# Gathering a chunk's small matmuls: one run of all scores and one of all outputs per chunk, in place of a run per unit

## The chip, the cores and the metric

The kernel runs on one core of one Trainium2 chip. The time is microseconds (us) of device time of one execution. A measurement is the median of several runs.

## The reference

A decayed linear attention, block by block with a carried state, feeds a two-layer network with a softplus between the layers. With B, H, S, D = 4, 8, 768, 64 and blocks of 64 rows:

```python
for b in range(nb):
    intra = np.einsum('bhic,bhjc->bhij', qb, kb) * Dmask[None]
    intra = np.einsum('bhij,bhjd->bhid', intra, vb)
    inter = np.einsum('bhid,bhde->bhie', qb * lam_pow[None], kv_state)
    out[:, :, sl] = intra + inter
    kb_dec = kb * rev_pow[None]
    kv_state = lam_block[None, :, None, None] * kv_state + np.einsum('bhsd,bhse->bhde', kb_dec, vb)
...
h = x @ w_in                                   # (3072, 512) @ (512, 2048)
g = np.maximum(h, 0.0) + np.log1p(np.exp(-np.abs(h)))
return (g @ w_out).astype(np.float32)          # (2048, 512)
```

## The kernel before

The sequence is cut into 6 chunks of 128 rows (`NCH`), each of two blocks of 64 rows. A chunk's attention is cut into 4 units (`NP`), each with two heads for all four batches; unit `g` belongs to chunk `g // 4`. A unit's q, k, k transposed and v come in one SBUF tile `att` of 1 MB in all, which the SyncE queue (SP) loads in two halves of 512 KB (`load_upto`, L86 to L89).

**Attention of a unit.** Chunk 0 has code of its own. For the later chunks, TensorE does 64x64 matmuls in fp32. `mm_scores` (L269 to L280) writes the scores into bank `x` (L276) and the state sums into bank `y` (L278). VectorE masks the scores (L297, into the tile of k) and updates the state with four `scalar_tensor_tensor` (L302). ScalarE first scales the transposed k (`k_decay`, L262), VectorE scales q (`q_decay`, L267). `mm_out` (L282 to L293) writes the unit's output `z` into the two banks of the `work` tile: L289 adds the part from the state, L293 the part from the masked scores. ScalarE copies `z` to the high half of x (`x_high`, L318), VectorE subtracts for the low half (`x_low`, L325). Every fp32 number is split into a high and a low fp32r half, so that each product of the network takes three matmuls.

**The network.** Per chunk there are 16 steps (`NF`), one per 128 columns of `w_in`. Step `s` does `mlp1(s)` (L353, 12 matmuls of 128x128 by 128x512 into a bank `h`), then softplus (ScalarE, L334), the high half (ScalarE, L338) and the low half (VectorE, L342), and 4 steps later (`LAG`) `mlp2` (L370, 12 matmuls) adds into the four `o` banks of the chunk. After a chunk's last `mlp2` the four banks are copied (ScalarE and VectorE, L376) and stored by SP (L378).

**The order** is written by hand: every engine executes its instructions as the code issues them. Up to step 16 a list of words sets it (the string before the loop), which also converts the weights. From step 17 a loop does it: at every fourth step an "event" `g` does the outputs of unit `g - 1` and at once the scores of unit `g` (`out1`, `sc1`), and then `mask`, `update_states`, `q_decay`, one extra `mlp2`, and asks for unit `g + 1`. So TensorE changes from large to small matmuls and back at each event: four times in the list for units 4 to 8, the last of them for units 7 and 8, and 16 times in the loop.

**PSUM** has 8 banks: four `o`, two `h`, two in `work`. SBUF tiles of 8 KB a partition (`b8`) number 22, of which 16 hold the weights.

Of the kernel before, what the change touches and what calls it, by code (L numbers as in the profile page):

```python
# [31 lines left out]
def decay_attention_softplus_ffn(  # L32
# [47 lines left out]
    def load_half(g, major):  # L80
        nc.sync.dma_start(out=unit(g)[:, major], in_=att[g // NP, g % NP, :, major])
# [4 lines left out]
    def load_upto(n):  # L86
        for g in range(len(units), min(n, NG)):
            for major in range(2):
                load_half(g, major)  # L89

# [56 lines left out]

    keep_warm(13)

# [131 lines left out]

    def mm_out(g, w):  # L282
        a, qd, v, st = k_of(g), q_of(g), vt_of(g), states[g]
        for b in range(B):
            cols = slice(b * 64, b * 64 + 64)
            for s in range(2):
                r = half(s)
                for t in range(2):
                    nc.tensor.matmul(w[half(t), s, cols], lhsT=st[r, b, t], rhs=qd[r, b, t], start=True, stop=False)  # L289
            for s in range(2):  # L290
                r = half(s)
                for t in range(2):
                    nc.tensor.matmul(w[half(t), s, cols], lhsT=v[r, b, t], rhs=a[r, b, t], start=False, stop=True)  # L293

# [13 lines left out]
    def update_states(g, y):  # L308
        u = y.rearrange("q (b t e) -> q b t e", b=B, t=2)
        st = states[g]  # L310
        decayed(g, st[hi], st[lo], lo, u[hi])
        if not last_chunk(g):
            states[g + NP] = th([128, B, 2, D], F32, f"st_{g + NP}")
            decayed(g, states[g + NP][lo], st[hi], hi, u[lo])

    def x_high(g, w):
# [41 lines left out]
    def mlp2(ss):  # L358
        c = ss[0] // NF
        ends = ss[-1] % NF == NF - 1  # L360
        if ss[0] % NF == 0:
            o_tiles[c] = [obank(f"o{c}_{b}") for b in range(B)]
        if ends:
            ob = t8([128, B, 512], F32, f"ob{c}")
        for b in range(B):
            for s in ss:
                f = s % NF
                g, w = g_tiles[s], w_of(f, 1)
                for n, (i, j) in enumerate(((0, 0), (0, 1), (1, 0))):
                    nc.tensor.matmul(  # L370
                        o_tiles[c][b], lhsT=g[:, i, b * 128 : (b + 1) * 128], rhs=w[:, j],
                        start=f == 0 and n == 0, stop=f == NF - 1 and n == 2,
                    )
            if ends:
                copy = nc.vector.tensor_copy if b % 2 else nc.scalar.copy
                copy(out=ob[:, b], in_=o_tiles[c][b])  # L376
                queue = nc.scalar if c == NCH - 1 and b % 2 == 0 else nc.sync
                queue.dma_start(out=out[b * S + c * C : b * S + (c + 1) * C, :], in_=ob[:, b])  # L378

# [82 lines left out]
    def out1(g):  # L462
        z[g] = work(f"z{g}")
        mm_out(g, z[g])

# [10 lines left out]
    for line in """  # L476
# [23 lines left out]
        glo 11, mlp 12, lo 22 23, sign 24 25, add 24 25, act 12, out1 6, sc1 7, m1 7, scale 26 27, shift 26  # L500
        27, ghi 12, round 28 29, hi 24 25, glo 12, kd1 8, sign 26 27, lo 24 25, mlp2 9, xh1 6, shift 28 29,
        mlp 13, load 32, round 26 27, act 13, add 26 27, scale 30 31, sign 28 29, hi 26 27, add 28 29, lo 26
        27, xl1 6, mlp2 10, mlp 14, hi 28 29, ghi 13, glo 13, round 30 31, mlp2 11, shift 30 31, act 14, qd
        7, ghi 14, glo 14, up 7, mlp 15, lo 28 29, act 15, sign 30 31, out1 7, ghi 15, sc1 8, up 8, add 30
        31, mlp2 12, mlp2 13, m1 8, xh1 7, unit 10, xl1 7, hi 30 31, mlp 16, lo 30 31, qd 8, glo 15
    """.replace("\n", " ").split(","):
# [8 lines left out]
    last = NCH * NF  # L515
    events = {s: 2 * NP + (s - NF) // 4 for s in range(NF, last - NF + 1, 4)}
    ahead = 17 - LAG
    for s in range(17, last + LAG):
        if events.get(s + 1, NG) < NG:
            run("kd1", events[s + 1])  # L520
        if s - 1 < last:
            chain_act(s - 1)
            chain_hi(s - 1)
            chain_lo(s - 1)
        if s == last + LAG - 2:
            mlp2([s - LAG, s - LAG + 1])
        elif s - LAG < last - 1 and ahead != s - LAG:
            mlp2([s - LAG])
        if s in events:
            g = events[s]  # L530
            run("out1", g - 1)
            if g < NG:
                run("sc1", g)
            run("xh1", g - 1)
            if g < NG:
                run("m1", g)
            if s % NF == 0:
                run("xl1", g - 1)
            if g < NG:
                run("up", g)  # L540
            if s % NF:
                run("xl1", g - 1)
            if g < NG:
                run("qd", g)
            ahead = s - LAG + 1
            mlp2([ahead])
            load_upto(g + 2)
        if s < last:
            mlp1(s)
# [37 lines left out]
```

## Time and profile before

| what | value |
|---|---|
| median of three runs | 595.82 us (595.77 to 595.89) |
| the profiled execution | 595.62 us; its span, first to last instruction, 593.8 us |
| TensorE matmuls, busy | 586.9 us, 99% of the span, 5009 records |
| TensorE weight loads, busy | 484.3 us, 82% |
| VectorE, ScalarE, busy | 224.3 us (38%), 210.0 us (35%) |
| granted TensorE clock | 1.000 over the span |
| DMA | 48.95 MB, mean 82 GB/s |

PE stands for TensorE's matmuls, PEld for its weight loads, DVE for VectorE, ACT for ScalarE. A written matmul of fp32 operands appears as two records of a matmul and two of a weight load (L276 has 640 matmul records for 20 units of 16 written ones); one of fp32r operands appears as one of each. The windows view gives, for a stretch of time, the busy time and the number of instructions (also those that only reach into it) of each engine, the granted clock, the mean busy share of the 16 DMA engines and the GB/s moved.

### The profile page before, as it was taken

What the parts mean: (1) busy time and instruction counts of PE and PEld (TensorE: products, weight loads), DVE (VectorE), ACT (ScalarE), POOL (GpSimd) and SP (SyncE); (2) the same over time, 40 slices, a digit from 0 to 9 for tenths busy, and PEclk for the clock granted to TensorE, in tenths of its full rate; (3) what the DMA queues carried; (4) which work ended last, traced back from release to release, by engine and by line L of the source; (5) the groups of instructions that cost most, each with busy time, mean ns of one, the idle gap of its engine ahead of it and who ended that gap; (6) DMA issues with size and microseconds to landing.
All of it is one profiled execution on the core that took longest, in us unless ns stands there. A gap on an engine that the chain in (4) does not pass through costs nothing.

```text
span 593.8 us, 11190 instructions
## 1 busy us (share of the span) xinstructions
PE 586.9 (99%) x5009; PEld 484.3 (82%) x5009; DVE 224.3 (38%) x338; ACT 210.0 (35%) x341; POOL 1.5 (0%) x9
## 2 busy tenths in 40 slices
PE   8999999999999999999999999999999999999997
PEld 6778888888888888888888888888888888888885
DVE  8999999623313134132232331312312211211011
ACT  5899867232233232322323213323232222222211
POOL 1000000000000000000000000000000000000000
PEclk9999999999999999999999999999999999999999
DMA  8999230214002106001022300220500000100001
GB/s 288 416 416 418 106 131 2 72 73 142 3 0 72 73 0 214 0 2 52 21 72 90 124 3 0 73 72 0 214 0 2 1 0 1 72 0 2 0 1 71
DMA packets 15759, 48.95 MB, mean 82 GB/s; under 512 B 1888, under 2 KB 1888, under 8 KB 15712
## 3 DMA queue, kind: packets, MB, share of 16 engines
q1 hardware_dynamic: 15344, 47.46, 21.4%
q10 hardware_dynamic: 368, 0.79, 0.4%
q8 instruction: 39, 0.64, 0.4%
q14 instruction: 8, 0.07, 0.0%
HBM read 41.95 MB, written 6.29 MB: 81 GB/s over the span
## 4 chain that ended last, share of the span: by engine, by line
PE 94%; DMA 3%; DVE 1%; SPq 1%; issue 0%; ACT 0%
PE o L370 45%; PE h L353 42%; PE x L276 2%; PE z L289 2%; PE z L293 2%; DMA att<-in_att 1%; DMA raw<-in_wts 1%; PE y L278 1%; DVE c L219 1%; DVE w L232 0%; DVE c L215 0%; DVE c L225 0%; PE y L440 0%; SPq L122 0%; PE w L276 0%
## 5 line engine op out<-in xcount | busy, mean ns | idle before, releaser
L370 PE MATMUL o<-w,g 128*128 128x512 f32 x1152 | 278.6, 392 | 0.0
L353 PE MATMUL h<-x,w 128*128 128x512 f32 x1152 | 274.5, 390 | 0.3 <-ACT x L417 0.3
L353 PEld LDWEIGHTS h<-x,w 128*128 128x128 f32 x1152 | 215.8, 188 | 46.4 <-DVE w L232 0.7
L370 PEld LDWEIGHTS o<-w,g 128*128 128x128 f32 x1152 | 214.8, 188 | 45.3
L342 DVE TENSOR_TENSOR g<-l,g 128x512 fp32r<-128x512 f32 x96 | 66.4, 692 | 305.3 <-ACT g L338 305.3
L334 ACT ACTIVATE l<-h 128x512 f32<-128x512 f32 x96 | 57.5, 598 | 310.9 <-PE h L353 308.6
L338 ACT CAST g<-l 128x512 fp32r<-128x512 f32 x96 | 59.6, 621 | 2.8
L302 DVE SCALAR_TENSOR_TENSOR st<-st,lam_c,y 64x256 f32<-64x256 f32 x68 | 29.9, 480 | 2.4 <-PE y L278 1.3
L297 DVE TENSOR_TENSOR att<-x,mask 128x512 f32<-128x512 f32 x19 | 13.1, 692 | 43.4 <-PE y L278 23.8
L318 ACT CAST x<-z 128x512 fp32r<-128x512 f32 x20 | 11.7, 585 | 41.4 <-PE z L293 41.4
L289 PEld LDWEIGHTS z<-att,st 64*64 64x64 f32 x640 | 17.0, 134 | 7.0 <-issue 6.3
L276 PE MATMUL x<-att 64*64 64x64 f32 x608 | 21.7, 219 | 0.0
L278 PE MATMUL y<-att 64*64 64x64 f32 x544 | 21.3, 219 | 0.0
L289 PE MATMUL z<-att,st 64*64 64x64 f32 x640 | 20.9, 224 | 0.0
L225 DVE CUSTOM_DVE_ANT_0 c<-raw,c 128x2048 uint16<-128x2048 uint16 (+1 forms) x19 | 20.0, 1054 | 0.3
L276 PEld LDWEIGHTS x<-att 64*64 64x64 f32 x608 | 20.1, 135 | 0.0
L232 DVE TENSOR_TENSOR w<-c,w 128x1024 fp32r<-128x1024 f32 (+1 forms) x19 | 20.0, 1055 | 0.1
L219 DVE SCALAR_TENSOR_TENSOR c<-raw,c 128x1024 uint32<-128x1024 uint32 (+1 forms) x19 | 20.0, 1053 | 0.0
L207 ACT ACTIVATE c<-raw 128x1024 f32<-128x1024 f32 (+1 forms) x19 | 18.9, 1006 | 3.1 <-DMA raw<-in_wts 3.1
L293 PE MATMUL z<-att 64*64 64x64 f32 x640 | 19.9, 218 | 0.0
L278 PEld LDWEIGHTS y<-att 64*64 64x64 f32 x544 | 19.6, 135 | 0.0
L211 ACT ACTIVATE raw<-raw 128x1024 uint32<-128x1024 uint32 (+1 forms) x19 | 19.1, 1013 | 1.2 <-DMA raw<-in_wts 1.2
(48 smaller groups left out, 172.6 us busy)
## 6 DMA issues: line engine op xcount, KB each, us to landing
att<-in_att SPq DMA_DIRECT2D x43, 512.0 KB, 4.9
raw<-in_wts SPq DMA_DIRECT2D x32, 512.0 KB, 9.2
out_dram<-ob SPq DMA_DIRECT2D x22, 256.0 KB, 2.3
att<-in_att SPq DMA_DIRECT2D x9, 256.0 KB, 7.5
out_dram<-ob ACTq DMA_DIRECT2D x2, 256.0 KB, 2.0
att<-in_att ACTq DMA_DIRECT2D x1, 256.0 KB, 4.7
lam_b<-in_lam SPq DMA_DIRECT2D x1, 4.0 KB, 2.8
```

Source lines behind the costliest of these rows:

```text
L219: nc.vector.scalar_tensor_tensor(out=c, in0=raw_at(ks, 1), scalar=0x80000000, in1=c, op0=ALU.bitwise_and, op1=ALU.bitwise_or)
L225: nc.vector.tensor_add(out=c, in0=c, in1=raw_at(ks, 0))
L276: nc.tensor.matmul(x[r, cols], lhsT=k[r, b, t], rhs=q[r, b, t], start=True, stop=True)
L278: nc.tensor.matmul(y[half(1 - s), cols], lhsT=kd[r, b, t], rhs=v[r, b, t], start=True, stop=True)
L289: nc.tensor.matmul(w[half(t), s, cols], lhsT=st[r, b, t], rhs=qd[r, b, t], start=True, stop=False)
L293: nc.tensor.matmul(w[half(t), s, cols], lhsT=v[r, b, t], rhs=a[r, b, t], start=False, stop=True)
L302: nc.vector.scalar_tensor_tensor(out=to[:, :, t], in0=of[:, :, t], scalar=lam_c[r, h : h + 1], in1=u[:, :, t], op0=ALU.mult, op1=ALU.add,)
L334: nc.scalar.activation(l_tiles[s], h_tiles.pop(s), AF.Softplus)
L338: nc.scalar.copy(out=g_tiles[s][:, 0, :], in_=l_tiles[s])
L342: nc.vector.tensor_sub(out=g[:, 1, :], in0=l_tiles.pop(s), in1=g[:, 0, :])
L353: nc.tensor.matmul(h_tiles[s], lhsT=w[:, i, cs], rhs=x[:, j, :], start=p == 0 and n == 0, stop=p == NP - 1 and n == 2,)
L370: nc.tensor.matmul(o_tiles[c][b], lhsT=g[:, i, b * 128 : (b + 1) * 128], rhs=w[:, j], start=f == 0 and n == 0, stop=f == NF - 1 and n == 2,)
```

## The change

Nothing of the arithmetic of chunks 1 to 5 changes. What changes is where the small matmuls of chunks 2 to 5 stand, and into which banks they write.

- **One run of scores per chunk.** At the fourth step of a chunk (`f == LAG - 1`), right behind the last `mlp2` of the chunk before, `chunk_scores` does the scores and state sums of all four units of the next chunk: into the two `h` banks, the four `o` banks (two units) and `work`. Behind it VectorE masks and updates for four units on end. The state of the chunk is kept in the unit's own tile, in the place of the transposed k (`update_kept`), for which ScalarE copies half of the old state.
- **One run of outputs per chunk.** At step 8 of a chunk (step 11 of the last but one) `chunk_outs` does the outputs of all four units of the next chunk: units 0 and 1 into the two `h` banks, units 2 and 3 into `work`. Four casts and four subtractions of 512 columns follow.
- **Loads.** From unit 8 on a unit is one transfer of 1 MB. Two units are asked for at a chunk's step 1 and two behind `chunk_outs`.
- **Stores.** The tile for a chunk's results is split in two of the `b4` tiles.
- **The `mlp2` order** follows `mlp2_upto`: none at step 4 of a chunk, two at step 5, one extra ahead of `chunk_outs`.
- **The start.** 13 large warm-up matmuls become 9 large and 34 small ones of 64x64 on zeros.
- **The list** loses `kd1 8`, `sc1 8`, `up 8`, `m1 8`, `qd 8`.

TensorE, in the middle of chunk 1, before: `z10` is the output of unit 10, `x11` and `y11` the scores and sums of unit 11, `o1_` the banks of `mlp2`, `h` those of `mlp1`.

```order
L370 MATMUL o1_3_1435<-w10_948,g24_1756 128x512 x3
L289 MATMUL z10_1851<-att10_1537,st_10_944 64x64 x4
L293 MATMUL z10_1851<-att10_1537 64x64 x4
...
L276 MATMUL x11_1884<-att11_1738 64x64
L278 MATMUL y11_1885<-att11_1738 64x64
...
L370 MATMUL o1_0_1432<-w11_997,g25_1774 128x512 x3
L370 MATMUL o1_1_1433<-w11_997,g25_1774 128x512 x3
L370 MATMUL o1_2_1434<-w11_997,g25_1774 128x512 x3
L370 MATMUL o1_3_1435<-w11_997,g25_1774 128x512 x3
L353 MATMUL h28_1943<-x_1_0_711,w10_948 128x512 x6
```

Now, the run of scores at chunk 2's step 3 (`x12` to `y15` are units of chunk 3, unit 15 in the `work` tile `w15`), and the run of outputs at its step 8 (`z3_0`, `z3_1` in the `h` banks, `z3_2568` in `work`):

```order
L422 MATMUL o1_3_1616<-w15_1307,g31_2104 128x512 x3
L290 MATMUL x12_2233<-att12_1887 64x64
L292 MATMUL y12_2234<-att12_1887 64x64
...
L290 MATMUL w15_2335<-att15_2134 64x64
L292 MATMUL w15_2335<-att15_2134 64x64
L405 MATMUL h35_2396<-x_2_0_1877,w1_295 128x512 x6
...
L422 MATMUL o2_3_2436<-w7_753,g37_2477 128x512 x3
L303 MATMUL z3_0_2566<-att12_1887 64x64 x2
L303 MATMUL z3_1_2567<-att12_1887 64x64 x2
...
L307 MATMUL z3_2568<-att15_2134 64x64 x4
L405 MATMUL h40_2711<-x_2_0_1877,w6_604 128x512 x6
```

A run of 128 pairs of a weight load and a matmul, of two units, has become two runs of 256 pairs, of four units each (192 in the scores of the last chunk), and of four places in a chunk at which TensorE changes to small matmuls two are left.

VectorE at the same place, before, at one event (`att13` masked, two states updated, `x_3_0` the low half, `att13` the scaled q):

```order
L342 TENSOR_TENSOR g35_2248<-l35_2246,g35_2248 128x512
L297 TENSOR_TENSOR att13_2141<-x13_2300,mask_104 128x512
L302 SCALAR_TENSOR_TENSOR st_13_1520<-st_13_1520,lam_c_108,y13_2301 64x4x64 x2
L302 SCALAR_TENSOR_TENSOR st_17_2339<-st_13_1520,lam_c_108,y13_2301 64x4x64 x2
L325 TENSOR_TENSOR x_3_0_2334<-z12_2267,x_3_0_2334 128x2x4x64
L267 TENSOR_TENSOR att13_2141<-att13_2141,lp_105 128x512
L342 TENSOR_TENSOR g36_2374<-l36_2372,g36_2374 128x512
```

and now, behind the run of scores:

```order
L428 COPY ob1_1_2212<-o1_3_1616 128x512
L311 TENSOR_TENSOR att12_1887<-x12_2233,mask_135 128x512
L316 SCALAR_TENSOR_TENSOR att12_1887<-st_12_1552,lam_c_139,y12_2234 64x4x64 x2
L316 SCALAR_TENSOR_TENSOR st_16_2372<-att12_1887,lam_c_139,y12_2234 64x4x64 x2
L311 TENSOR_TENSOR att13_1889<-x13_2267,mask_135 128x512
...
L311 TENSOR_TENSOR att15_2134<-w15_2335,mask_135 128x512
L316 SCALAR_TENSOR_TENSOR att15_2134<-st_15_1573,lam_c_139,w15_2335 64x4x64 x2
L316 SCALAR_TENSOR_TENSOR st_19_2393<-att15_2134,lam_c_139,w15_2335 64x4x64 x2
L394 TENSOR_TENSOR g35_2411<-l35_2409,g35_2411 128x512
L281 TENSOR_TENSOR att12_1887<-att12_1887,lp_136 128x512
```

Five instructions that stood apart for each unit now stand on end for four units, ahead of the low half `g35`.

The diff, cut to its core:

```diff
     def load_upto(n):
         for g in range(len(units), min(n, NG)):
-            for major in range(2):
-                load_half(g, major)
+            if g < 2 * NP:
+                for major in range(2):
+                    load_half(g, major)
+            else:
+                nc.sync.dma_start(out=unit(g), in_=att[g // NP, g % NP])
...
-    keep_warm(13)
+    warm_h = bank("warm_h")
+
+    def keep_warm_small(n):
+        zero = warm.bitcast(F32)
+        for k in range(n):
+            r, other = half(k % 2), k // 2 % 2
+            c = half((k + other) % 2)
+            nc.tensor.matmul((warm_ps, warm_h)[other][c, :64], lhsT=zero[r, :64], rhs=zero[r, :64], start=True, stop=True)
+
+    keep_warm(9)
+    keep_warm_small(34)
...
+    def update_kept(g, y):
+        u = y.rearrange("q (b t e) -> q b t e", b=B, t=2)
+        old, st = states[g], kt_of(g)
+        states[g] = st
+        nc.scalar.copy(out=st[lo], in_=old[lo])
+        decayed(g, st[hi], old[lo], lo, u[hi])
+        if not last_chunk(g):
+            states[g + NP] = th([128, B, 2, D], F32, f"st_{g + NP}")
+            decayed(g, states[g + NP][lo], st[hi], hi, u[lo])
+
+    def chunk_scores(c):
+        homes = [(bank, bank), (obank, obank), (obank, obank), None]
+        for g, home in zip(range(c * NP, c * NP + NP), homes):
+            if home:
+                xy[g] = [new(f"{name}{g}") for new, name in zip(home, "xy")]
+            else:
+                w = work(f"w{g}")
+                xy[g] = w[:, 0], w[:, 1]
+            mm_scores(g, *xy[g])
+
+    def chunk_outs(c):
+        homes = {0: [bank(f"z{c}_{s}") for s in range(2)]}
+        w = work(f"z{c}")
+        homes[1] = [w[:, s] for s in range(2)]
+        for p in range(NP):
+            mm_out(c * NP + p, homes[p // 2], p % 2 * 256)
+        for i in range(2):
+            x_of(c, 2 * i)
+            x = x_tiles[c, i].rearrange("q n p (b s i) -> q n s p b i", b=B, s=2)
+            of = [home.rearrange("q (p b i) -> q p b i", p=2, b=B) for home in homes[i]]
+            for s in range(2):
+                nc.scalar.copy(out=x[:, 0, s], in_=of[s])
+            for s in range(2):
+                nc.vector.tensor_sub(out=x[:, 1, s], in0=of[s], in1=x[:, 0, s])
...
-            ob = t8([128, B, 512], F32, f"ob{c}")
+            ob = [t4([128, 2, 512], F32, f"ob{c}_{i}")[:, j] for i in range(2) for j in range(2)]
...
     for s in range(17, last + LAG):
-        if events.get(s + 1, NG) < NG:
-            run("kd1", events[s + 1])
+        c, f = divmod(s, NF)
+        first = (c + 1) * NP
+        if f == 1 and c < NCH - 1:
+            load_upto(first + NP)
+        if 1 <= f <= 3 and c < NCH - 1:
+            for g in ((first,), (first + 1,), (first + 2, first + 3))[f - 1]:
+                run("kd1", g)
...
+        if f != LAG or c == NCH:
+            mlp2_upto(s - LAG)
+        if f == LAG - 1 and c < NCH - 1:
+            chunk_scores(c + 1)
+            for g in range(first, first + NP):
+                mask_scores(g, xy[g][0])
+                update_kept(g, xy[g][1])
+        if f in range(LAG, 2 * LAG) and c < NCH - 1:
+            run("qd", first + f - LAG)
+        if f == (11 if c == NCH - 2 else 8) and c < NCH - 1:
+            if c < NCH - 2:
+                mlp2_upto(s - LAG + 1)
+            chunk_outs(c + 1)
+            mlp2_upto(s - LAG + 1)
+            load_upto(first + NP + 2)
         if s < last:
             mlp1(s)
```

More of the change, by code (lines that the diff above doesn't have):

```diff
@@ L280, in mm_scores, with mm_out @@
                         )
-    def mm_out(g, w):
+    def mm_out(g, w, first=0):
         a, qd, v, st = k_of(g), q_of(g), vt_of(g), states[g]
         for b in range(B):
-            cols = slice(b * 64, b * 64 + 64)
+            cols = slice(first + b * 64, first + b * 64 + 64)
             for s in range(2):
@@ L288, in mm_out @@
                 for t in range(2):
-                    nc.tensor.matmul(w[half(t), s, cols], lhsT=st[r, b, t], rhs=qd[r, b, t], start=True, stop=False)
+                    nc.tensor.matmul(w[s][half(t), cols], lhsT=st[r, b, t], rhs=qd[r, b, t], start=True, stop=False)
             for s in range(2):
@@ L292, in mm_out @@
                 for t in range(2):
-                    nc.tensor.matmul(w[half(t), s, cols], lhsT=v[r, b, t], rhs=a[r, b, t], start=False, stop=True)
+                    nc.tensor.matmul(w[s][half(t), cols], lhsT=v[r, b, t], rhs=a[r, b, t], start=False, stop=True)
     def mask_scores(g, x):
@@ L375, in mlp2 @@
                 copy = nc.vector.tensor_copy if b % 2 else nc.scalar.copy
-                copy(out=ob[:, b], in_=o_tiles[c][b])
+                copy(out=ob[b], in_=o_tiles[c][b])
                 queue = nc.scalar if c == NCH - 1 and b % 2 == 0 else nc.sync
-                queue.dma_start(out=out[b * S + c * C : b * S + (c + 1) * C, :], in_=ob[:, b])
+                queue.dma_start(out=out[b * S + c * C : b * S + (c + 1) * C, :], in_=ob[b])
     def w_group(j):
@@ L463, in out1 @@
         z[g] = work(f"z{g}")
-        mm_out(g, z[g])
+        mm_out(g, [z[g][:, s] for s in range(2)])
     step = {
@@ L500, in decay_attention_softplus_ffn @@
         glo 11, mlp 12, lo 22 23, sign 24 25, add 24 25, act 12, out1 6, sc1 7, m1 7, scale 26 27, shift 26
[L501 to L505, printed above, removed]
+        27, ghi 12, round 28 29, hi 24 25, glo 12, sign 26 27, lo 24 25, mlp2 9, xh1 6, shift 28 29, mlp 13,
+        load 32, round 26 27, act 13, add 26 27, scale 30 31, sign 28 29, hi 26 27, add 28 29, lo 26 27, xl1
+        6, mlp2 10, mlp 14, hi 28 29, ghi 13, glo 13, round 30 31, mlp2 11, shift 30 31, act 14, qd 7, ghi
+        14, glo 14, up 7, mlp 15, lo 28 29, act 15, sign 30 31, out1 7, ghi 15, add 30 31, mlp2 12, mlp2 13,
+        xh1 7, unit 10, xl1 7, hi 30 31, mlp 16, lo 30 31, glo 15
     """.replace("\n", " ").split(","):
@@ L515, in decay_attention_softplus_ffn, with mlp2_upto @@
     last = NCH * NF
-    events = {s: 2 * NP + (s - NF) // 4 for s in range(NF, last - NF + 1, 4)}
-    ahead = 17 - LAG
-    for s in range(17, last + LAG):
-        if events.get(s + 1, NG) < NG:
-            run("kd1", events[s + 1])
+    done = 17 - LAG
+    def mlp2_upto(n):
+        nonlocal done
+        while done < n:
+            ss = [done + 1] if done + 1 < last - 2 else [done + 1, done + 2]
+            if ss[-1] > n:
+                break
+            mlp2(ss)
+            done = ss[-1]
+    for s in range(17, last + LAG):
+        c, f = divmod(s, NF)
[5 more added lines that the diff above has]
+                run("kd1", g)
         if s - 1 < last:
@@ L524, in decay_attention_softplus_ffn @@
             chain_lo(s - 1)
[L525 to L547, printed above, removed]
+        if f != LAG or c == NCH:
[13 more added lines that the diff above has]
+            load_upto(first + NP + 2)
         if s < last:
```

## The prediction

> **What bounds the kernel now.** I read the page first: busy shares, then the chain that ended last.
>
> ```profile
> PE 586.9 (99%) x5009; PEld 484.3 (82%) x5009; DVE 224.3 (38%) x338; ACT 210.0 (35%) x341; POOL 1.5 (0%) x9
> PE 94%; DMA 3%; DVE 1%; SPq 1%; issue 0%; ACT 0%
> L370 PE MATMUL o<-w,g 128*128 128x512 f32 x1152 | 278.6, 392 | 0.0
> L353 PE MATMUL h<-x,w 128*128 128x512 f32 x1152 | 274.5, 390 | 0.3 <-ACT x L417 0.3
> ```
>
> TensorE is the bound: it is in 94% of the chain, and its groups have next to no idle time ahead of them. So a change pays only if TensorE has less to do or passes from one thing to the next faster. A busy time of 392 ns overlaps its neighbours, so I take cadences from the timeline of PE, in one stretch of the loop:
>
> ```profile
> 194.00 2.88 PE L353 MATMUL h<-x,w 128*128 128x512 f32 x12
> 196.72 2.88 PE L370 MATMUL o<-w,g 128*128 128x512 f32 x12
> ...
> 205.25 0.30 PE L289 MATMUL z<-att,st 64*64 64x64 f32 x8
> 205.37 0.30 PE L293 MATMUL z<-att 64*64 64x64 f32 x8
> 205.48 0.30 PE L289 MATMUL z<-att,st 64*64 64x64 f32 x8
> 205.60 0.30 PE L293 MATMUL z<-att 64*64 64x64 f32 x8
> ```
>
> Twelve large matmuls start 2.72 us before the next twelve: 226.7 ns each. Eight small ones take 0.117 us (0.35 us over three rows): 14.6 ns each. The windows view, cut at one stretch of large matmuls and the run of small ones behind it, and the timeline at the last run, which has outputs alone:
>
> ```profile
> 182.99:204.97 21.98, 21.98 (x102) 17.94 (x97) 6.51 (x11) 5.69 (x10) 0.00 (x0) 1.00 0.28 96
> 204.97:207.02 2.05, 2.05 (x130) 1.98 (x129) 0.00 (x0) 0.58 (x1) 0.00 (x0) 1.00 0.02 6
> ...
> 493.52 0.34 PE L289 MATMUL z<-att,st 64*64 64x64 f32 x8
> ...
> 494.61 3.02 PE L370 MATMUL o<-w,g 128*128 128x512 f32 x12
> ```
>
> Between two events lie 96 large matmuls (four steps of 24): 96 x 0.2267 = 21.76 us, measured 21.98, so 0.22 us is lost at the two ends of the stretch. The run of small ones has 128 (64 for a unit's output, 64 for a unit's scores): 128 x 0.0146 = 1.87 us, measured 2.05, so 0.18 is lost there. The run of 64 at the end takes 1.09 us against 0.93: 0.16 lost. So a passage to small matmuls and back costs 0.22 + 0.16 = 0.38 us however long the run, and the switch from one unit's work to another's inside a run 0.02 us.
>
> **The change part by part.**
>
> *Passages.* From the event for units 7 and 8 on, before has 17 passages; after has 1 (the output of unit 7 alone, in the list) and 2 in each of 4 chunks, so 9. Removed: 8 x 0.38 = 3.0 us. Inside the longer runs there are 8 x 3 switches of unit in place of 16: 8 x 0.02 = 0.2 us more. The count of small matmuls stays. Sum: 2.8 us less on TensorE, all of it on the path, since nothing else ends later there.
>
> *The run's instructions.* This is the cost that before does not show. The page and the windows view at a run:
>
> ```profile
> q8 instruction: 39, 0.64, 0.4%
> ...
> 349.25:350.20 0.95, 0.95 (x65) 0.95 (x66) 0.00 (x0) 0.00 (x0) 0.00 (x0) 1.00 0.03 9
> 350.20:351.20 1.00, 1.00 (x80) 1.00 (x70) 0.00 (x0) 0.58 (x1) 0.00 (x0) 1.00 0.08 16
> 351.20:351.60 0.40, 0.40 (x13) 0.33 (x4) 0.20 (x1) 0.00 (x0) 0.00 (x0) 1.00 0.00 0
> ```
>
> 39 packets of 0.64 MB are 16 KB each, and 5009 weight loads with 5009 matmuls make 10,018 instructions: 257 a packet. I read a packet as a piece of 256 TensorE instructions, fetched while the one before it is worked off. Of small matmuls a piece is 128 pairs, 1.87 us; of large ones 128 x 0.2267 = 29 us. In the run that starts at 349.25 one piece of 16 KB comes with the rows from 350.20 on; the share 0.08 of 16 engines is 1.28 us of one engine, so it is there by about 351.5, 2.3 us into the run. That run begins 138 instructions into a piece, counting those of the built program; the eight new runs begin at 128, 142, 136, 150, 144, 158, 152 and 155, which is what the small warm-up matmuls do to the count, so this run shows their first fetch. Before, a run is one piece long and ends at 351.3, so a late piece meets large matmuls, which use 9 instructions a us. The new runs need it in their middle: after 1.87 us, or later by as much as lies queued on TensorE. Bounds for one run: 0, or 2.3 - 1.87 = 0.43 us; earlier fetch is no gain, since nothing waited for it. For the four runs of outputs nothing else is on the DMA engines then (the loads behind them take the place of units that the run reads, and start 3 us into it), and I take 0 for them: they begin 4 to 20 instructions further into their piece than the run of the rows, and since large matmuls use 9 instructions a us, their fetch starts 0.4 to 2 us earlier against the run. The four runs of scores stand right behind the chunk's last `mlp2`, so the stores run beside them. Before, at the end of chunk 2:
>
> ```profile
> 318.95 2.16 SPq L378 DMA_DIRECT2D out_dram<-ob  x4
> ...
> 319.70:320.80 1.10, 1.10 (x6) 0.94 (x5) 0.75 (x2) 0.11 (x1) 0.00 (x0) 1.00 0.76 289
> 320.80:321.70 0.90, 0.90 (x5) 0.74 (x5) 0.00 (x0) 0.00 (x0) 0.00 (x0) 1.00 1.07 403
> 321.70:324.00 2.30, 2.30 (x11) 1.89 (x11) 0.09 (x1) 1.22 (x2) 0.00 (x0) 1.00 0.44 167
> ```
>
> The engines are full for some 2 us just when the piece is wanted. The wait is between 0.43 and, behind all of that traffic, 0.43 + 2.0 us. I take 0.33 for three of them (a fetch that comes between the stores, and instructions in hand that cover part) and 0 for the last, which begins at 152, so that its fetch starts some 1.5 us earlier. Sum: 3 x 0.33 = 1.0 us. Bounds for all eight: 0, and 4 x 0.43 + 4 x 2.43 = 11.4 us.
>
> [...]
>
> *VectorE and ScalarE behind the scores.* The rows of one event, and of a copy of 64x512:
>
> ```profile
> 126.68 1.52 DVE L376 COPY ob<-o 128x512 f32<-128x512 f32 x2
> 134.06 0.58 ACT L318 CAST x<-z 128x512 fp32r<-128x512 f32 x1 [2.59 <-PE z L293]
> 134.98 0.69 DVE L297 TENSOR_TENSOR att<-x,mask 128x512 f32<-128x512 f32 x1 [2.78 <-PE x L276]
> 135.71 1.80 DVE L302 SCALAR_TENSOR_TENSOR st<-st,lam_c,y 64x256 f32<-64x256 f32 x4
> 137.53 0.69 DVE L325 TENSOR_TENSOR x<-z,x 128x512 fp32r<-128x512 f32 x1
> 144.51 0.91 ACT L262 ACTIVATE att<-att,rp 128x256 f32<-128x256 f32 x2
> 6.64 1.25 ACT L188 COPY mask<-spare 64x512 f32<-64x512 f32 x2 [2.52 <-DVE spare L176]
> ```
>
> Counted from the start of the run of scores (4.0 us long): the copy of the last `o` bank is done at 0.76, and that bank is first written at 2.0, for unit 2's scores. VectorE masks unit 0 from 1.0 on and each unit takes 0.69 + 1.80 = 2.5 us, so the units are done at 3.5, 6.0, 8.5 and 11.0. `mlp1` right behind the run needs the bank of unit 0's scores (free at 1.7, wanted at 4.0), the next `mlp1` that of its sums (3.5, wanted at 6.8); then the two `mlp2` of step 5 take the four `o` banks, free at 4.2, 6.0, 6.7 and 8.5 and wanted from 9.5 to 11.5. Here the missing `mlp2` of step 4 is the cover; with it the banks would be wanted 2.7 us sooner, and TensorE would wait. The low half that queues behind the 11.0 us is done at 11.7 and wanted by `mlp2` at some 23. ScalarE's four extra copies of 0.63 us and its `k_decay` (0.91 a unit) lie in 65% of idle time. All of that: 0; without its cover up to 3 us a chunk.
>
> *Behind the outputs.* Unit 0's and 1's outputs are complete half-way, at 1.9 us; the cast ends at 2.6, the subtraction at 3.3, and `mlp1` wants the bank at 4.0. Zero, with 0.7 us to spare; if VectorE came late, some 0.5 us a chunk.
>
> *Loads.* Two units, 2 MB, have moved in 7.8 us, and the first of the second pair is asked for some 19 us ahead of its scores (steps 0, 1, 2 at 5.44 us and an `mlp2`):
>
> ```profile
> 325.50:333.30 7.80, 7.80 (x155) 6.69 (x144) 3.74 (x7) 0.85 (x2) 0.00 (x0) 1.00 0.78 271
> ```
>
> That hides it, as one transfer or as two; the stores stand behind the loads on SP, not ahead of them. Zero; if the buffers came 10 us late, TensorE would wait for the rest.
>
> *The start.* Scores of unit 0 wait for a load, not for the warm-up:
>
> ```profile
> 1.45 4.62 PE L146 MATMUL warm_ps<-warm 128*128 128x512 f32 x13 [1.45 <-DVE warm L141]
> 6.88 1.16 PE L396 MATMUL x<-att 64*128 64x128 f32 x16 [0.82 <-DMA att<-in_att]
> 1.45:4.44 2.99, 2.99 (x7) 2.41 (x8) 1.51 (x3) 1.75 (x2) 0.68 (x2) 1.00 0.55 116
> ```
>
> The first seven start 0.427 us apart, so nine end near 4.9 us; 68 small ones add 1.0 us at 14.6 ns, or 2.0 at half that rate: 5.9 to 6.9, against 6.88. Zero; at worst 0.2 us.
>
> Sum on the profiled execution of 595.62 (span 593.8 and 1.8 around it): 595.6 - 2.8 + 1.0 = 593.8. The median of the runs shown is 0.2 above it, so I predict 594.0.
>
> **The rivals.** A difference under 0.2% (1.2 us) is about what a measurement of this kernel cannot tell from none.
>
> *Pieces are never late.* The fetch works further ahead than one piece, or the instructions that TensorE has in hand cover 0.4 us. For it: no run of before shows a gap in its middle. Then 595.8 - 2.8 = 593.0. [...]
>
> *Late pieces eat the gain.* Each of the eight runs waits 0.35 us on average, inside the bounds above, or a bank is late behind the outputs: 8 x 0.35 = 2.8, so 595.8.
>
> *Late pieces cost more than the passages.* The place is the middle of each run; the price is 0.43 us in runs of outputs and, with most of the stores ahead of the fetch, 0.43 + 1.4 in runs of scores: 4 x 0.43 + 4 x 1.83 = 9.0, so 595.8 - 2.8 + 9.0 = 602.0. From 0.5 us a run on (4.0 in all) the kernel is slower by more than 1.2 us. For it: the 2.3 us of the row at 350.20 against 1.87. Against it: the runs of outputs and the last two of scores begin later in the piece than that run, and TensorE has instructions in hand.
>
> *The gathering itself makes a new wait* for a bank is part of the second rival: by the counts above each bank has 0.7 us or more.
>
> **How the numbers follow.** Forecast 594.0: chance 0.42, its own range 593.4 to 594.6. Never late, 593.0: 0.20. Eaten, about 595.8: 0.20. Slower, about 602: 0.18. Faster by over 0.2% holds the first two: 0.62; within 0.2%: 0.20; slower: 0.18. The range runs from 592.6 (nothing late, and 0.4 us that the passages may cost more) to 597.0 (the third case to its end), and leaves out most of the slower case.
>
> **What would show it.** Right: two runs of small matmuls per chunk of about 4.0 us, with the stretches of large ones at 226.7 ns each; in the runs of scores a gap of some tenths of a us near their middle, ended by "issue" and not by an engine, and a 16 KB fetch just ahead of it; none in the runs of outputs. Wrong: runs over 4.5 us; TensorE waiting for VectorE or ScalarE at the first `mlp1` behind a run or at the `mlp2` of step 5; scores waiting for a load; or a first score later than 6.9 us.

## The result and the profile after

The changed kernel takes 601.39 us (median of 6 runs, 600.96 to 603.06) against 595.76 us (595.22 to 595.89) of the kernel before: the ratio is 1.0103, 95% interval 1.0089 to 1.0118. It is slower by 5.6 us, where I forecast 1.8 us faster. The outcome is the rival "Late pieces cost more than the passages" (602.0).

The page of after, to set beside the four rows of before (the profiled execution took 602.93 us, its span is 601.1):

```profile
PE 586.0 (97%) x5073; PEld 486.4 (81%) x5073; DVE 223.6 (37%) x338; ACT 219.2 (36%) x357; POOL 1.5 (0%) x9
q8 instruction: 40, 0.66, 0.4%
PE 97%; issue 1%; DVE 1%; DVEq 0%
L290 PE MATMUL x<-att 64*64 64x64 f32 x480 | 16.2, 220 | 5.7 <-issue 5.7
L307 PE MATMUL z<-att 64*64 64x64 f32 x640 | 19.8, 219 | 1.2 <-issue 1.2
```

TensorE is as busy as before (586.0 against 586.9 us) in a span 7.3 us longer, so it stands still for 8.2 us more (15.1 against 6.9). The two groups of small matmuls now have idle time ahead of them, and its releaser is "issue": no engine and no load was waited for. The waits of PE, complete:

```profile
PE x L290 <- issue: 5.7, 3, 2.2
PE z L463 <- DVE w L246: 1.9, 1, 1.9
PE warm_ps L149 <- DVE warm L144: 1.4, 1, 1.4
PE z L307 <- issue: 1.2, 1, 1.2
PE z L303 <- issue: 1.0, 1, 1.0
```

Five waits for "issue", three in runs of scores (L290), two in runs of outputs; the other two rows belong to the start. No row names VectorE or ScalarE behind a run. The windows view over the eight long runs, scores and outputs in turn (each from its first matmul to the first large one behind it):

```profile
127.95:134.23 6.28, 4.12 (x258) 3.92 (x257) 5.57 (x11) 1.87 (x4) 0.00 (x0) 1.00 0.48 175
164.37:169.73 5.36, 4.15 (x257) 4.00 (x256) 1.29 (x2) 1.07 (x2) 0.00 (x0) 1.00 0.03 6
227.08:232.97 5.89, 4.21 (x258) 4.01 (x257) 5.19 (x11) 1.87 (x4) 0.00 (x0) 1.00 0.50 183
263.15:268.31 5.16, 4.20 (x257) 4.00 (x256) 1.29 (x2) 1.07 (x2) 0.00 (x0) 1.00 0.02 6
325.66:331.68 6.02, 4.12 (x258) 3.92 (x257) 5.32 (x11) 1.87 (x4) 0.00 (x0) 1.00 0.49 179
361.84:365.73 3.89, 3.89 (x258) 3.82 (x257) 1.15 (x2) 1.07 (x2) 0.00 (x0) 1.00 0.02 4
423.08:426.96 3.88, 3.88 (x193) 3.81 (x192) 3.24 (x6) 1.87 (x4) 0.00 (x0) 1.00 0.71 269
470.71:474.74 4.03, 4.03 (x257) 3.96 (x257) 1.28 (x2) 1.07 (x2) 0.00 (x0) 1.00 0.01 4
sum 40.51, PE 32.61 PEld 31.45 DVE 24.32 ACT 11.78 POOL 0.00; mean PE 4.08 PEld 3.93 DVE 3.04 ACT 1.47 POOL 0.00
```

A run that does not stop takes 3.89 us (the sixth), and TensorE is busy from end to end of it; the first five take 5.16 to 6.28, with PE busy for 4.1 to 4.2 of that. (The seventh, of 192 pairs, takes 3.88 us without a stop, in tuned42 below as well: by the trace its instructions pass at some 9.6 ns each, where those of the other runs take 7.3. The eighth is 0.14 us over the sixth.) Inside one run of outputs, cut where its piece of instructions moves and where TensorE stops:

```profile
164.37:165.50 1.13, 1.13 (x77) 1.13 (x80) 0.00 (x0) 0.00 (x0) 0.00 (x0) 1.00 0.00 0
165.50:166.64 1.14, 1.14 (x93) 1.14 (x84) 0.00 (x0) 0.14 (x1) 0.00 (x0) 1.00 0.06 14
166.64:168.04 1.40, 0.21 (x13) 0.13 (x6) 0.92 (x2) 0.93 (x2) 0.00 (x0) 1.00 0.00 0
168.04:169.73 1.69, 1.67 (x103) 1.60 (x102) 0.37 (x1) 0.00 (x0) 0.00 (x0) 1.00 0.04 10
```

The second column from the right is the mean share of the 16 DMA engines: 0.06 of 1.14 us is 1.1 us of one engine, the packet of 16 KB. It is over by 166.64. That is when TensorE stops, and it goes on only at 168.04, 1.40 us later, with nothing on the DMA engines in between. In a run of scores the stores lie ahead of the packet:

```profile
227.08:228.80 1.72, 1.72 (x117) 1.72 (x120) 1.18 (x2) 0.54 (x2) 0.00 (x0) 1.00 0.89 341
228.80:229.42 0.62, 0.62 (x56) 0.62 (x44) 0.59 (x2) 0.31 (x2) 0.00 (x0) 1.00 1.09 400
229.42:231.30 1.88, 0.20 (x12) 0.07 (x4) 1.82 (x5) 0.41 (x1) 0.00 (x0) 1.00 0.31 111
231.30:232.97 1.67, 1.67 (x101) 1.60 (x101) 1.61 (x5) 0.62 (x1) 0.00 (x0) 1.00 0.08 22
```

The engines are full until TensorE stops, and the stop is longer, 1.88 us. Number all of TensorE's records in the trace from the first on (weight loads, matmuls and its few semaphore instructions), and start again at 0 after every 256 (after has 10,198 such records and 40 packets of 16 KB, 255 to a packet): I call this number the place of an instruction. In all five stops the last instruction ahead of the gap has place 191 or 192, which I read as the edge between two pieces. By this count the eight runs start at places 127, 141, 135, 149, 143, 157, 151 and 154 of a piece (one lower than the prediction's count, and the last three are those that do not stop). A run of 256 pairs is two pieces long and so has two edges in it; these five pass the first without a stop, and stop at the second, 2.2 to 2.35 us in.

### The profile page after: what moved, and what is told of

Same layout as the page of the kernel before. It is cut to its first block, busy times and chain, and to the rows that moved or that the text cites. A ratio compares the mean times of both kernels' runs of the same rounds, so it can differ in the third digit from the quotient of the medians.

```text
span 601.1 us, 11358 instructions
## 1 busy us (share of the span) xinstructions
PE 586.0 (97%) x5073; PEld 486.4 (81%) x5073; DVE 223.6 (37%) x338; ACT 219.2 (36%) x357; POOL 1.5 (0%) x9
## 4 chain that ended last, share of the span: by engine, by line
PE 97%; issue 1%; DVE 1%; DVEq 0%
PE h L405 44%; PE o L422 44%; PE x L290 2%; PE z L303 2%; PE z L307 2%; PE z L463 1%; PE warm_ps L149 1%; PE x L448 1%; PE w L290 1%; PE y L292 0%; PE y L492 0%; PE warm_ps L159 0%; DVE att L454 0%; PE w L292 0%; DVE w L246 0%
## 5 line engine op out<-in xcount | busy, mean ns | idle before, releaser
L422 PE MATMUL o<-w,g 128*128 128x512 f32 x1152 | 275.1, 390 | 0.0
L290 PE MATMUL x<-att 64*64 64x64 f32 x480 | 16.2, 220 | 5.7 <-issue 5.7
L290 PEld LDWEIGHTS x<-att 64*64 64x64 f32 x480 | 15.0, 135 | 7.6 <-issue 7.6
L366 DVE TENSOR_TENSOR x<-z,x 128x512 fp32r<-128x512 f32 x16 | 10.3, 685 | 28.9 <-ACT x L364 28.9
L307 PE MATMUL z<-att 64*64 64x64 f32 x640 | 19.8, 219 | 1.2 <-issue 1.2
L364 ACT CAST x<-z 128x512 fp32r<-128x512 f32 x16 | 8.6, 589 | 28.2 <-PE z L307 28.2
L307 PEld LDWEIGHTS z<-att 64*64 64x64 f32 x640 | 17.8, 135 | 1.3 <-issue 1.3
L242 ACT CAST w<-c 128x1024 fp32r<-128x1024 f32 (+1 forms) x19 | 17.3, 914 | 3.1 <-DVE c L239 3.0
L276 ACT ACTIVATE att<-att,rp 128x256 f32<-128x256 f32 x40 | 17.7, 499 | 0.0
L303 PE MATMUL z<-att 64*64 64x64 f32 x512 | 16.0, 220 | 1.0 <-issue 1.0
L303 PEld LDWEIGHTS z<-att 64*64 64x64 f32 x512 | 14.4, 135 | 2.5 <-issue 2.5
```

The lines of the kernel that those rows point to most:

```text
L290: nc.tensor.matmul(x[r, cols], lhsT=k[r, b, t], rhs=q[r, b, t], start=True, stop=True)
L303: nc.tensor.matmul(w[s][half(t), cols], lhsT=st[r, b, t], rhs=qd[r, b, t], start=True, stop=False)
L307: nc.tensor.matmul(w[s][half(t), cols], lhsT=v[r, b, t], rhs=a[r, b, t], start=False, stop=True)
L422: nc.tensor.matmul(o_tiles[c][b], lhsT=g[:, i, b * 128 : (b + 1) * 128], rhs=w[:, j], start=f == 0 and n == 0, stop=f == NF - 1 and n == 2,)
```

## The experiments

Theory A: a piece is asked for some way ahead of its edge; where TensorE passes small matmuls all that way, the piece comes too late, so the place at which a run starts decides. Rival B: a long run has a wait of its own, wherever it starts. Rival C: the stores are the cause. The first four kernels ran beside each other on one chip (before there: 595.91), the next four on another occasion (before: 595.70), the last two on a third (before: 595.98). "Places" are counted as above.

**small40.** Six small warm-ups more, 24 instructions:

```diff
-    keep_warm_small(34)
+    keep_warm_small(40)
```

> The changed kernel with 40 small warm-up matmuls in place of 34, which moves every later instruction of TensorE by 24. Theory A, late pieces: in the changed kernel a run waits in its middle (1.2 to 2.4 us, five runs of eight, 8.9 us in all) where it begins at 127 to 149 of a piece of 256 instructions, and not where it begins at 151 to 157; with 24 more all eight begin at 151 to 179, so none waits: 601.4 - 8.9 = 592.5 us, each run of 256 pairs about 3.9 us. Theory B, the gathering makes a wait of its own (banks, engines, the length of the run) wherever it stands in a piece: 601.4 us, five waits as before. Theory C, the stores beside the scores are the cause: only the two runs of outputs could be mended by the shift, 598.8.

Measured: 593.54 us (593.21 to 593.75), ratio 0.9961 [0.9946, 0.9976]. The first run of scores, a later run of outputs, and the sum over the eight:

```profile
127.00:131.95 4.95, 4.21 (x258) 4.00 (x257) 4.28 (x9) 1.87 (x4) 0.00 (x0) 1.00 0.61 222
...
352.65:356.54 3.89, 3.89 (x257) 3.82 (x256) 1.14 (x2) 1.07 (x2) 0.00 (x0) 1.00 0.02 4
...
sum 32.17, PE 31.43 PEld 30.76 DVE 18.59 ACT 11.78 POOL 0.00; mean PE 3.93 PEld 3.85 DVE 2.32 ACT 1.47 POOL 0.00
```

Twenty-four empty instructions at the start, the long runs untouched, and the kernel is 7.9 us faster than after and faster than before. The sum of the runs falls from 40.51 to 32.17 us. Only the run at place 151 still stops, for 0.94 us, where I had expected none to. B falls here.

**small36.** The same with 36, 8 instructions.

```diff
-    keep_warm_small(34)
+    keep_warm_small(36)
```

> The changed kernel with 36 small warm-up matmuls in place of 34: 8 instructions later. Runs of scores begin at 135, 143, 151, 159 and runs of outputs at 149, 157, 165, 162 of their piece. Theory A: the scores at 135 and 143 wait as runs at these places did before (1.9 and 2.1 us), the outputs at 149 wait 1.2, the others nothing: 592.5 + 5.2 = 597.7 us. Theory B: 601.4. Theory C: four runs of scores, of which three wait some 2 us: 598.8 or more.

Measured: 598.98 us (597.50 to 600.80), ratio 1.0052 [1.0031, 1.0073]. Three runs stop, at places 135 (2.00), 149 (1.71) and 143 (1.94 us). The runs that the two extra warm-ups moved from 149 and 143 to 157 and 151 no longer do (the second still takes 4.07 us).

**large13.** Before's warm-ups, the rest as after; places 255 to 29.

```diff
-    keep_warm(9)
-    keep_warm_small(34)
+    keep_warm(13)
```

> The changed kernel with the 13 large warm-up matmuls of before and no small ones: runs begin at 255 to 29 of a piece, so that the boundary lies 1.2 to 1.4 us into a run and the next one 1.9 us behind it, still inside. Theory A: every one of the eight runs asks for a piece only after it began and waits 1.2 us or more (less than 2 us where the stores have passed): 592.5 + 8 x 1.3 = 602.9 us, 602 to 605, the waits at the second boundary, some 3.2 us into the run. Theory B: five waits, 601.4. At the start of the kernel nothing lost and nothing gained.

Measured: 605.42 us (603.89 to 606.91), ratio 1.0161 [1.0140, 1.0181]. The median is 0.4 us over the range that I gave, and seven of eight runs stop, where I had expected all eight to (the seventh, of 192 pairs, ends ahead of its second edge). The stops take 1.35 to 2.04 us, 3.1 to 3.3 us into the run: they lie further in, since the second edge lies further in. The first outputs run (place 13) again stops with its piece's packet, which is in the first row, already over:

```profile
162.40:165.60 3.20, 3.20 (x217) 3.20 (x217) 0.45 (x1) 1.07 (x2) 0.00 (x0) 1.00 0.02 5
165.60:166.96 1.36, 0.22 (x14) 0.14 (x6) 0.84 (x2) 0.00 (x1) 0.00 (x0) 1.00 0.31 48
```

So without the small warm-ups the gathered runs cost even more.

**nostore.** The results of chunks 0 to 4 are not stored; all else as after.

```diff
-                queue.dma_start(out=out[...], in_=ob[b])
+                if c == NCH - 1:
+                    queue.dma_start(out=out[...], in_=ob[b])
```

> The changed kernel without the stores of the results of chunks 0 to 4 (left out of the output), so that nothing else moves on the DMA engines beside the runs of scores; the places in the pieces stay. Theory A: the waits of the scores (2.4, 1.9, 2.1 us) fall to those of the outputs, which stand alone (1.2 to 1.4), and the outputs' stay: 601.4 - 2.3 = 599.1 us. Theory C, the stores are the cause: the waits of the scores vanish, 595.1. Theory B: 601.4.

Measured: 599.24 us (598.59 to 599.77), ratio 1.0057 [1.0042, 1.0072]. The scores runs still stop, for 1.26, 1.10 and 1.28 us in place of 2.36, 1.88 and 2.10. The second of them:

```profile
224.73:227.07 2.34, 2.34 (x157) 2.34 (x156) 1.76 (x3) 0.84 (x3) 0.00 (x0) 1.00 0.03 7
227.07:228.18 1.11, 0.21 (x13) 0.07 (x5) 1.08 (x4) 0.41 (x1) 0.00 (x0) 1.00 0.00 0
```

The share of DMA ahead of the stop is 0.03 in place of 0.89 and more. The stores make a stop 0.8 to 1.1 us longer; they do not make it. The outputs at places 141 and 149 stop much as in after (1.31 and 1.37 us for 1.41 and 1.16), and the run at place 154, which goes through in after, stops for 0.36 us here: that place is at the limit. C falls as the cause, and stays as a part.

**small42.** 42 small warm-ups, to clear the run at place 151.

```diff
-    keep_warm_small(34)
+    keep_warm_small(42)
```

> 42 small warm-ups instead of 34, 32 more TensorE instructions ahead of the first run than in after, so that every long run starts at places 159 to 189 of a 256-instruction piece (151 to 181 with 40). Theory A (the place where a run starts decides; a piece asked for from inside the run comes too late): the 0.94 us that the first scores run still lost with 40 goes, two small warm-ups add 0.06, all eight runs take 3.89 us (2.9 for the one of 192 pairs or 3.88 with its passage): 592.7 us, 592.3 to 593.1. Rival (that 0.94 is the first long run's own, whatever its place): 593.6.

Measured: 594.43 us (593.54 to 596.01), ratio 0.9983 [0.9974, 0.9991]. A miss: all eight runs take 3.89 us, as expected, yet the time rose by 0.9 us. The timeline of PE behind the run of outputs that starts at 351.38, at place 189:

```profile
355.05 0.30 PE L307 MATMUL z<-att 64*64 64x64 f32 x8
355.27 0.50 PE L405 MATMUL h<-x,w 128*128 128x512 f32 x1
356.83 0.85 PE L405 MATMUL h<-x,w 128*128 128x512 f32 x3 [1.06 <-issue]
```

A run from place 189 has its first two edges 3 and 259 instructions in, and ends 3 instructions short of a third. The large matmuls behind it meet that edge instead: 1.06 us. The run of place 186 loses 0.4 us the same way. The stop moves out of the run, so that the sum over the runs no longer shows it.

**small48.** More of the same: places 183 to 213.

```diff
-    keep_warm_small(34)
+    keep_warm_small(48)
```

> 48 small warm-ups: long runs start at places 183 to 214. Theory A, on the other side: where a run starts after the edge at 192, its second edge comes 5 to 21 instructions before its end, and the piece for it is asked for 1.4 to 1.5 us into the run, so the run stands still for 1 to 2 us right before its end, at about 3.7 us: up to five such runs, 4 to 7 us in all, 597 to 600 us. Runs that start before 192 lose nothing. Rival (only runs that start before place 150 lose time; more padding than 40 is as good as 40): 593.7 us.

Measured: 603.76 us (602.71 to 604.53), ratio 1.0135 [1.0121, 1.0149]. Six of eight runs stop, 0.95 to 1.74 us, 3.6 to 3.7 us in; the seventh with 192 pairs ends short of its edge; behind the run of place 183 the large matmuls lose 1.1 us. I had expected "up to five" and 597 to 600: a run from place 191 also stops, and the one from 183 loses time behind itself. The windows of one run:

```profile
163.07:166.80 3.73, 3.73 (x253) 3.73 (x254) 0.98 (x2) 1.07 (x2) 0.00 (x0) 1.00 0.02 4
166.80:168.26 1.46, 0.22 (x13) 0.09 (x6) 0.31 (x1) 0.00 (x0) 0.00 (x0) 1.00 0.70 135
```

With three pairs of the run to go it stands still for 1.46 us. There is one good stretch of places, and it has two sides.

**before_warm.** Before, with after's 9 large and 34 small warm-ups and nothing else.

```diff
-    keep_warm(13)
+    keep_warm(9)
+    keep_warm_small(34)
```

> Before, with only the warm-ups changed: 9 large and 34 small ones instead of 13 large. This has nothing of the long runs; it moves the first fetch of a piece from 18 us to about 10.5 us, amid the first loads. Theory S (that fetch holds up one load of data by 1.5 us, and all that follows starts 1.5 us later): the first output run starts at about 12.6 instead of 11.1 us, and the time is 597.0 to 597.4 us. Prediction on record (the start costs nothing, at worst 0.2): 595.8 to 596.0. A change of place of before's own 128-pair runs may add or take up to 1 us; their stalls are read off one by one.

Measured: 595.70 us (595.25 to 597.07, 11 runs), ratio 1.0005 [0.9996, 1.0014]. Theory S falls for the median: the warm-ups by themselves cost nothing there. But 3 of 11 executions took 596.90 to 597.07, about what theory S gave (more on them under "The start" below). The first piece does come earlier (its packet begins at 10.9 us in place of 18.0, by the traces), and TensorE idles more from 12 to 16 us (PE busy 2.66 of 4.00 us; before 3.96), but by its first run of 128 pairs the kernel is only 0.28 us behind:

```profile
12.00:16.00 4.00, 2.66 (x31) 1.89 (x29) 4.00 (x8) 1.46 (x3) 0.00 (x0) 1.00 1.03 411
```

```profile
53.08 0.34 PE L300 MATMUL z<-att,st 64*64 64x64 f32 x8
```

None of its runs of 128 pairs stops, at places from 9 to 254.

**before_load.** Before, with after's loads of 1 MB.

```diff
-            for major in range(2):
-                load_half(g, major)
+            if g < 2 * NP:
+                for major in range(2):
+                    load_half(g, major)
+            else:
+                nc.sync.dma_start(out=unit(g), in_=att[g // NP, g % NP])
```

> Before, with only the loads changed: one load of 1 MB for each unit from unit 8 on instead of two of 512 KB. Prediction on record and theory A: no difference, 595.6 to 596.1 us. Rival (longer packets hold up the pieces of instructions, or a unit lands later): over 596.4.

Measured: 595.31 us (594.93 to 595.42), ratio 0.9993 [0.9984, 1.0003]. The loads cost nothing, as predicted; the time is 0.3 us under my range.

**split13.** large13, with each outputs run cut in two by a second-layer step that stood beside it.

```diff
-    def chunk_outs(c):
+    def chunk_outs(c, n):
...
         for p in range(NP):
+            if p == 2:
+                mlp2_upto(n)
             mm_out(c * NP + p, homes[p // 2], p % 2 * 256)
...
-            if c < NCH - 2:
-                mlp2_upto(s - LAG + 1)
-            chunk_outs(c + 1)
-            mlp2_upto(s - LAG + 1)
+            chunk_outs(c + 1, s - LAG + 1)
```

> large13 (all warm-ups large, every run loses 1.35 to 2.04 us, 605.4 us) with each outputs run cut into two of 128 pairs by moving the second-layer step that stood ahead of it (or behind it, for the last) into its middle. Theory A (a run is late where its second edge is reached before the piece asked for some 300 instructions earlier can be used): a run of 256 instructions with 2.9 us of large matmuls behind it gives each piece 4.9 us, so the four output stalls of large13 (1.35, 1.36, 1.41 and 1.56, 5.7 us in all) go, four passages of 0.38 come, the scores runs keep theirs: 601.3 us, 600.0 to 602.5. Rival (the loss is one of the edge itself at this place of the program, however long the run): 605.4 + 1.5 = 606.9.

Measured: 599.42 us (599.29 to 601.81), ratio 1.0065 [1.0049, 1.0081], 0.6 us under my range (I had started from the median of large13; from its profiled 603.89 the same sum gives 599.7). The outputs do not stop any more; the first of them:

```profile
159.69:161.71 2.02, 2.02 (x129) 1.95 (x128) 0.00 (x0) 0.00 (x0) 0.00 (x0) 1.00 0.00 0
161.71:164.66 2.95, 2.95 (x18) 2.18 (x13) 1.29 (x2) 1.08 (x2) 0.00 (x0) 1.00 0.02 6
164.66:166.68 2.02, 2.02 (x129) 1.96 (x128) 0.00 (x0) 0.00 (x0) 0.00 (x0) 1.00 0.03 8
```

The scores runs, which were not cut, still stop for 1.73, 1.94 and 1.72 us. The same instructions at nearly the same places, with 2.95 us of large matmuls between the halves: it is the length without a pause that is late, not the edge.

**tuned42.** small42, with one outputs run put ahead of the second-layer step and the last one begun a loop step earlier and behind one more second-layer step; places 159 to 183.

```diff
-        if f == (11 if c == NCH - 2 else 8) and c < NCH - 1:
-            if c < NCH - 2:
+        if f == (10 if c == NCH - 2 else 8) and c < NCH - 1:
+            if c != NCH - 3:
```

> 42 small warm-ups with two of the four output runs moved back by one second-layer step (24 instructions), the last of them begun one step of the loop earlier, so that all eight runs start at places 159 to 183 instead of 159 to 189. Theory A (a run from 189 or 186 ends 3 or 6 instructions short of its second edge, and the large matmuls behind it stand still for the piece: 1.3 and 0.7 us in small42): both stalls go, small42's 594.2 becomes 592.3, 592.0 to 593.0. Rival (small42's two stalls are the chance of those fetches): 594.2.

Measured: 592.50 us (592.15 to 592.68), ratio 0.9937 [0.9923, 0.9951]. It is the fastest kernel of the study, 3.5 us under before. The run that had stopped behind its end in small42 (now at place 165), the 1.63 us behind it, and in a fence of their own the first run and the sum over all eight:

```profile
348.98:352.87 3.89, 3.89 (x257) 3.82 (x257) 1.14 (x2) 1.07 (x2) 0.00 (x0) 1.00 0.02 4
352.87:354.50 1.63, 1.63 (x13) 1.36 (x8) 0.53 (x2) 1.08 (x2) 0.00 (x0) 1.00 0.84 201
```

```profile
127.07:130.96 3.89, 3.89 (x257) 3.82 (x256) 3.24 (x7) 1.87 (x4) 0.00 (x0) 1.00 0.75 276
...
sum 31.11, PE 31.11 PEld 30.58 DVE 17.54 ACT 11.78 POOL 0.00; mean PE 3.89 PEld 3.82 DVE 2.19 ACT 1.47 POOL 0.00
```

PE is busy for 31.11 of 31.11 us; no run stops.

**The sum.** If the stops are all that tells these kernels apart, each should take tuned42's 592.50 and what its eight runs take over 31.11 us (with what small42 and small48 lose behind runs, and 0.22 us of large matmuls for each passage that split13 adds):

| kernel | runs in all, us | 592.50 + excess | measured |
|---|---|---|---|
| after | 40.51 | 601.9 | 601.39 |
| small36 | 37.19 | 598.6 | 598.98 |
| small40 | 32.17 | 593.6 | 593.54 |
| small42 | 31.11, and 1.5 behind | 594.0 | 594.43 |
| small48 | 39.65, and 1.1 behind | 602.1 | 603.76 |
| large13 | 42.79 | 604.2 | 605.42 (profiled: 603.89) |
| nostore | 38.25 | 599.6 | 599.24 |
| split13 | 37.26 | 599.5 | 599.42 |

Six of eight agree within some 0.5 us. The runs come from one execution and the measurements are medians, and executions of the kernels with many stops differ by 1 to 3 us.

## Why the prediction was wrong

**The step that failed is "The run's instructions".** I saw what decides: a piece of 256 instructions, runs two pieces long, a fetch asked for too late, and the stops are where I said they would show, near the middle, ended by "issue". I had its size wrong, in one term. "The share 0.08 of 16 engines is 1.28 us of one engine, so it is there by about 351.5" took the end of the packet for the time from which TensorE can use it. The runs show some 1.4 us from the one to the other (166.64 to 168.04, with an idle DMA; 1.25 to 1.50 us over the five stops of after, 1.16 to 1.58 us over the 34 stops of more than 0.3 us in all the traces). So the bound "0, or 2.3 - 1.87 = 0.43 us" for a run was no bound. Its 1.87 was off too, the other way: the second piece is wanted at the second edge, which the runs of after that stop reach 2.2 to 2.35 us in. Without the 1.4 us the row of before would have given next to no wait. How much instructions in hand cover, which I counted on, no run shows: the rows of the stops have TensorE busy for 0.20 to 0.22 us, and then it stands still. Corrected it is: packet over about when the edge is reached, 2.3 us into the run, plus 1.4.

- *Runs of outputs, taken as 0.* Two of four stop, 1.41 and 1.16 us (places 141, 149); two do not (157, 154). The argument for the 0, that a later start fetches earlier, holds only from a certain place on. By the trace the packet begins 1.21 and 1.18 us into the runs at 141 and 149, no earlier than in the run of before (0.99 us, place 137), and 0.30 and 0.36 us ahead of the runs at 157 and 154. The zero of the run at 154 is in part luck: in nostore the packet of that run begins 0.25 us into it, and it stops.
- *Runs of scores, taken as 0.33.* Three lose 2.36, 1.88 and 2.10 us; the last, taken as 0, loses none. Its packet does begin earlier, 0.30 us ahead of the run, as I argued. But its slower instructions, of which I said nothing, help: it reaches its second edge 2.86 us in, where a run of 256 pairs from the same place is there at 2.22 us and stopped for 0.94 us in small40 and lost 0.2 us in small36. Of that the stores make 0.8 to 1.1 us (nostore), inside the 0 to 2.0 that I gave them; the rest is again the 1.4.
- *In sum* 1.0 us was predicted, and the runs take 40.51 - 31.11 = 9.4 us more than they need. The bound for all eight, 11.4 us, held the sum, though the 0.43 us for each run of outputs did not hold. Given that bound, and no row of before that speaks of TensorE going on within a run two pieces long, a chance of 0.18 for the slower rival was too low. That before shows no stop in its runs was no evidence on that: none of them is over one piece long.

**The slower rival had the sum, not the shares.** Its 9.0 us came from 0.43 for each of four outputs and 1.83 for each of four scores. Measured are 1.16 and 1.41 for two outputs, and 1.9 to 2.4 for three scores. That 602.0 came so near to 601.39 is luck.

**Passages: right in kind, somewhat low.** From the first run of 128 pairs on, where the two kernels stand alike, to the end of the span (593.8 and 590.9 us), before takes 541.0 us and tuned42 537.3. Of before and of tuned42:

```profile
52.80 0.34 PE L289 MATMUL z<-att,st 64*64 64x64 f32 x8
```

```profile
53.61 0.34 PE L303 MATMUL z<-att,st 64*64 64x64 f32 x8
```

That is 3.7 us for 8 passages, if nothing else tells these two apart, where 3.0 less 0.2 was predicted: 0.46 each in place of 0.38. The 0.2 for more switches of unit is not there: a run of 256 pairs takes 3.89 us, 0.15 over 256 x 0.0146, no more than a run of 128.

**VectorE, ScalarE, banks, loads: right.** No wait of after names them, the casts and subtractions included, and before_load measures the loads at no difference.

**The start: right in the median.** before_warm gives 595.70 against 595.70. "At worst 0.2" was wrong: three of its executions were 1.2 to 1.4 us longer than the median. In after's profiled execution the clock is low for a while at the start:

```profile
12.00:16.00 4.00, 3.29 (x30) 2.99 (x32) 2.13 (x5) 1.47 (x3) 0.00 (x0) 0.61 1.03 412
```

It took 602.93 us where four of the six took 600.96 to 601.47. By the trace the clock is 0.50 from 12.92 to 16.33 us, with TensorE busy all that while; half of these 3.41 us, 1.7 us, is an estimate of what it cost. The mean clock of that execution is 0.996. The three long executions of before_warm have 0.996 or 0.997 as well (its other eight 0.999 or 1.000), but no trace of them was kept. Three of four executions of large13 and one of four of split13 have it too, and both start with before's 13 large warm-ups, so the small warm-ups are not all of it. What sets the clock low was not tried, and stays open.

**Together**, -3.7 of passages and +9.4 of stops are +5.7 us, against 5.6 measured. Both terms come from single executions, so they agree better than they can vouch for.

**The rival of 593.0, pieces never late,** holds for one stretch of places alone: runs of 512 instructions went through unstopped every time only from places 157 to 181 in these kernels (of those from 151 and 154 some stopped). tuned42, whose runs of 512 all start there, takes 592.50.

## What to carry to other kernels

A row of very short instructions, 7.3 ns each here, can have a price that a busy share does not show: the eight runs of after took 40.51 us, those of tuned42 31.11, and TensorE's busy time was 97% of the span all the same. Where a run of them is longer than one piece of 256, count at which place of a piece it starts (157 to 181 went through here), and look at the time between the end of the packet and the next instruction (some 1.4 us here), not only at the packet. If it stops, a few empty instructions far ahead of it, or one slower step in its middle, were cheap mends here: 24 instructions at the start were worth 7.9 us, a second-layer step in the middle of each outputs run (2.95 us in the first) 4.6 us (the profiled executions of large13 and split13, 603.89 and 599.29), and a reordered kernel without stops 8.9. The mend by empty instructions holds for one program only: eight more warm-ups than in small40 cost 10.2 us (small48), and whatever adds or takes instructions ahead of a run moves its place (eight warm-ups moved it by 32).

## What the runs showed of the hardware that was not expected

- In the stops TensorE went on at a piece's edge some 1.4 us after the packet of 16 KB had moved (1.40 us in the outputs run shown, with no DMA beside it; 1.25 to 1.50 us over the five stops of after). What fills this time the runs do not show.
- Count packets and edges off one for one, and in after no packet begins more than 297 instructions ahead of its edge; 12 of 40 begin 291 to 297 ahead, be it 2.4 us before the edge (the second of the run at place 157) or 33.4 us (the edge at 595.01, among large matmuls). So I estimate that a piece is asked for some 300 instructions ahead, by count and not by time. In runs that stop the packet begins nearer, 143 and 135 instructions ahead in the outputs runs at 141 and 149. Ahead of a run of tuned42 that starts at place 181, the packet for its second edge moves among large matmuls, in the second of these windows:

```profile
251.50:252.70 1.20, 1.20 (x7) 0.97 (x7) 0.36 (x1) 0.78 (x2) 0.00 (x0) 1.00 0.00 0
252.70:253.80 1.10, 1.10 (x6) 0.92 (x5) 0.34 (x1) 0.00 (x0) 0.00 (x0) 1.00 0.05 15
253.80:256.39 2.59, 2.59 (x12) 1.88 (x10) 0.00 (x0) 0.00 (x0) 0.00 (x0) 1.00 0.00 0
```

  It begins at 252.76 by the trace, 3.6 us or 30 instructions ahead of the run, at place 151, and the edge is 297 further. In the other seven runs of tuned42 the edge is 287 to 297 instructions behind the start of the packet. Of small instructions at 7.3 ns, 300 are 2.2 us, less than the packet's 1.1 and the 1.4 behind it; of large ones at 0.113 us they are 34 us.
- A stop can fall behind the run that causes it, on a large matmul (1.06 us in small42), where no one would look for an instruction that came late.
- With the stores on the DMA engines (a share of 0.89 and 1.09 ahead of the stop shown) the three stops of the scores runs were 0.8 to 1.1 us longer than in nostore (0.03).
